# Chunked attention before two gated layers: heads traded in half a block, value products in four quadrants of the array

## The chip, the cores and the metric

The kernel runs on one core of a Trainium2 chip. The metric is the device time of one execution in microseconds (us): before the change 1714.94 us, the median of 3 runs (1713.28 to 1716.34). The profile is of one further execution.

## The reference, cut to what matters

```python
def _attn_ref(q, k, v):                       # each 8 batches x 8 heads x 576 rows x 64
    q_c, k_c, v_c = (x.reshape(B, H, S // 64, 64, D) for x in (q, k, v))   # chunks of 64 rows
    scores = (1.0 / np.sqrt(D)) * np.matmul(q_c, k_c.transpose(0, 1, 2, 4, 3))
    scores = scores - np.max(scores, axis=-1, keepdims=True)
    attn = np.exp(scores)
    attn = attn / (np.sum(attn, axis=-1, keepdims=True) + 1e-09)
    return np.matmul(attn, v_c).reshape(B, H, S, D)

x = attn.transpose(0, 2, 1, 3).reshape(4608, 512)                          # heads side by side
x = (1.0 / (1.0 + np.exp(-(x @ w_gate))) * (x @ w_val)) @ w_out            # 512 -> 1536 -> 512
h = x @ w2_in                                                              # 512 -> 2048
out = np.where(h >= 1, h, np.where(h <= -1, 0.0, (h + 1) ** 2 / 4)) @ w2_out
```

Each head attends within chunks of 64 rows alone, so a chunk of one head is a 64x64 score matrix, a softmax over its rows and a 64x64 value product. All matmuls of the two layers are computed as three products of a high and a low part each.

## The kernel before, in words

**Stages.** The 4608 rows are cut into nine blocks of 512. Blocks 0 to 3 and 5 to 8 are the first 512 rows of a batch each; block 4 (`REST`) holds the last 64 rows of all eight batches. In the first stage, TensorE goes through the blocks; for each it makes 24 projections of the block's attention output X (12 gate, 12 value), one to a *slot*: twelve matmuls of 128x512 (function `three`, L459 to L461). A sigmoid on ACT (L875) and a product on DVE (L878) follow, and the result goes to DRAM (`g_store`, L761). While block b is projected, the attention of block b + 1 is made between the projections, and the weights of the later layers are prepared on DVE, ACT and GpSimd (POOL) and spooled to DRAM (`w_load` L103 and L107, `w_low` L112, `w_bits`, `w_join`, `s_sums`, `s_split` L170, `s_spool` L182). The second layers follow later with other code, which the change doesn't touch.

**Attention of one pair of heads.** Eight heads make four pairs. The class `Whole` has a method for each step, named by one letter:
- `load`: q and k of the two heads, from DRAM, all issued on SP (L284; block 4 L263). In form "V" the partition is 32 times a group (head, half of the head's 64 columns) plus the row modulo 32, and each DMA fills one group of one of q and k: eight DMAs of 64 KB.
- `t`: DVE transposes 32x32 squares (L304), so that head h has its 64 columns on partition half h and the rows along the tile.
- `s` (S): 16 score matmuls of 64x64x64 in fp32, for each chunk and head, from partition half h (row group of the array) to the partition half of the chunk's parity (column group), into a bank for each head. One fp32 matmul is two instructions in the trace.
- `m`, `e`, `n`, `w`: row maximum and subtraction (DVE, L331 and L333), exponent (ACT, L338), sum and reciprocal (DVE, L343 to L346), scaling (POOL, L351).
- `p` (PT): four 128x128 transposes on TensorE (L357). `c`: ACT copies them from PSUM (L360).
- `o` (O): 16 value matmuls of 64x64x64 (L367): head h from partition half h to partition half h, into a bank of its own.
- `x`: ACT copies the two halves of 64x512 into X's high part (L375). `l`: DVE takes the low part (L380).
- `v_load`: two DMAs, one for each head (L297): key row within the chunk on the partitions of that head's half.

**The order is written out.** `later_block(b, starts, when)` gives for each pair a start slot and for each of the letters t s m e n w p c o x l an offset in slots; `at(slot, prio, ...)` files the step, and `emit(slot)` issues a slot's steps ahead of its projection, sorted by the fraction of the slot, then priority, then order of filing. s, p and o have priority 0, m, e, c and x 1, the others 3; loads have a fraction of 0.5. Each engine, SP too, works its own instructions in the order of issue. Pairs start 5 slots apart in block 1 (during block 0's projections) and 6 apart later; `load` stands two pairs ahead. The scores use banks b4 and b5, PT b6, O b6 and b7. Block 0's own attention comes before all projections, in an order written out in `ORDER` and `LOADS`, with forms "M", "V", "M", "T" for its four pairs; in M and T TensorE transposes rather than DVE.

Of the kernel before, what the change touches and what calls it, by code (L numbers as in the profile page):

```python
# [13 lines left out]
AF = mybir.ActivationFunctionType  # L14
ALU = mybir.AluOpType
# [14 lines left out]
def kernel(  # L30
# [15 lines left out]
    nc = tc.nc  # L46
    P = 128
    B, H, S, D = q.shape
# [3 lines left out]
    KT = DM // P  # L52
    CH = 64
    BS = 512
# [23 lines left out]
    def f32(t):  # L78
        return t.bitcast(F32)
# [138 lines left out]
    def x_tile(n=BS, name="x"):  # L218
        return pool["x"].tile([P, 2, n], F32R, tag="x", name=name, bufs=8)

    REST = NB // 2
    RS = S - BS

    def batch(blk):
        return blk - (blk > REST)

    NC = BS // P
    heads = [slice(h * D, (h + 1) * D) for h in range(2)]
    chunks = [slice(i * CH, (i + 1) * CH) for i in range(BS // CH)]

    class Whole:
# [7 lines left out]
        def bank(self, i, shape, name):  # L239
# [4 lines left out]
                self.nt += 1  # L244
            return ps.tile(shape, F32, tag=tag, name=name)

        def load(self, p):
            t = self.alloc("qk")
            how = self.how[p]
            if how == "V":  # L250

                t = t.rearrange("p i (t r) -> p i t r", r=32)
            elif how == "T":

                t = t.rearrange("p i (j h d) -> p i j h d", h=2, d=D)
            else:
                t = t.rearrange("p i (h j d) -> p i h j d", h=2, d=D)
            for i, src in enumerate((q, k)):
                if self.b == REST:
                    for g in range(4):  # L260
                        h, j = divmod(g, 2)
                        for c in range(RS // 32):
                            nc.sync.dma_start(  # L263
                                out=t[32 * g:32 * g + 32, i, c::RS // 32],
                                in_=src[:, 2 * p + h, BS + 32 * c:BS + 32 * c + 32, 32 * j:32 * j + 32].rearrange(
                                    "b i r -> i b r"
                                ),
                            )
                else:
                    rows = src[batch(self.b), 2 * p:2 * p + 2, :BS]  # L270
                    if how == "M":
                        nc.sync.dma_start(
                            out=t[:, i].rearrange("i h j d -> i h (j d)"),
                            in_=rows.rearrange("h (i j) d -> i h (j d)", j=NC),
                        )
                    elif how == "T":
                        for h in range(2):
                            nc.sync.dma_start(
                                out=t[:, i, :, h], in_=rows[h].rearrange("(i j) d -> i j d", j=NC)
                            )  # L280
                    else:
                        for g in range(4):
                            h, j = divmod(g, 2)
                            nc.sync.dma_start(  # L284
                                out=t[32 * g:32 * g + 32, i],
                                in_=rows[h, :, 32 * j:32 * j + 32].rearrange("(t i) r -> i t r", i=32),
                            )
            self.qk[p] = t

        def v_load(self, p):  # L290
            self.V[p] = t = self.alloc("vd").rearrange("p i (c e) -> p (i c) e", e=D)
            for h, hs in enumerate(heads):
                if self.b == REST:
                    rows = v[:, 2 * p + h, BS:].rearrange("b k d -> k b d")
                else:
                    rows = v[batch(self.b), 2 * p + h, :BS].rearrange("(c k) d -> k c d", k=CH)
                nc.sync.dma_start(out=t[hs, :BS // CH], in_=rows)  # L297

        def t(self, p):
            qk, how, ident = self.qk[p], self.how[p], kv_["ident"]  # L300
# [14 lines left out]
        def s(self, p):  # L315
            t = self.T[p]
            self.SP[p] = self.alloc("sp")
            banks = [self.bank(1 + h, [P, NC, CH], "S") for h in range(2)]
            for c, ts in enumerate(chunks):
                for h, hs in enumerate(heads):  # L320
                    nc.tensor.matmul(  # L321
                        banks[h][heads[c % 2], c // 2], lhsT=t[hs, 0, ts], rhs=t[hs, 1, ts], start=True, stop=True
                    )
            self.B["s", p] = banks

        def m(self, p):
            s = self.SP[p][:, 0].rearrange("p (g h k) -> p g h k", h=2, k=CH)
            m = cp.tile([P, 2, NC], F32, tag="m0", name="m", bufs=2)
            banks = self.B.pop(("s", p))
            for h, b in enumerate(banks):  # L330
                nc.vector.tensor_reduce(out=m[:, h], in_=b, axis=AX.X, op=ALU.max)  # L331
            for h, b in enumerate(banks):
                nc.vector.tensor_tensor(  # L333
                    out=s[:, :, h], in0=b, in1=m[:, h].unsqueeze(2).to_broadcast([P, NC, CH]), op=ALU.subtract
                )

        def e(self, p):
# [10 lines left out]
        def w(self, p):  # L348
            s = self.SP[p][:, 0].rearrange("p (g k) -> p g k", k=CH)
            r = self.B.pop(("r", p))  # L350
            nc.gpsimd.tensor_tensor(out=s, in0=s, in1=r.unsqueeze(2).to_broadcast([P, 2 * NC, CH]), op=ALU.mult)  # L351
# [9 lines left out]

        def o(self, p):

            banks = [self.bank(4 + h, [P, BS], "O") for h in range(2)]
            for c, ts in enumerate(chunks):
                for h, hs in enumerate(heads):
                    nc.tensor.matmul(  # L367
                        banks[h][hs, ts], lhsT=self.V[p][hs, c], rhs=self.SP[p][hs, 1, ts], start=True, stop=True
                    )
            self.B["o", p] = banks  # L370

        def x(self, p):
            t = X[self.b, p] = x_tile()
            for h, hs in enumerate(heads):
                nc.scalar.activation(t[hs, 0], self.B["o", p][h][hs], AF.Copy)  # L375

        def l(self, p):
            t = X[self.b, p]
            for (h, hs), b in zip(enumerate(heads), self.B.pop(("o", p))):
                nc.vector.tensor_tensor(out=t[hs, 1], in0=b[hs], in1=f32(t[hs, 0]), op=ALU.subtract)  # L380

    def first_block():
        ft = ps.tile([P, BS], F32, tag="b5", name="fill")
# [55 lines left out]
    def later_block(b, starts, when):  # L439

        bufs = {"qk": 3, "qkT": 1, "sp": 2, "vd": 2}

        def alloc(nm):
            cols = BS // 2 if nm == "vd" else BS
            return pool["u"].tile([P, 2, cols], F32, tag=nm, name=nm, bufs=bufs[nm])

        a = Whole(b, [None, "b4", "b5", "b6", "b6", "b7"], alloc, "V" * KT)
        for p, s0 in enumerate(starts):
            at(begun[-2] + 0.5, 5, a.load, p)
            begun.append(s0)  # L450
            at(s0 + 0.5, 5, a.v_load, p)
            for fn, dt in zip("tsmenwpcoxl", when):
                at(s0 + dt, {"s": 0, "p": 0, "o": 0, "m": 1, "e": 1, "c": 1, "x": 1}.get(fn, 3), getattr(a, fn), p)
# [22 lines left out]
    banks, B0, B1, OP, R_ = {}, {}, {}, {}, {}  # L476
# [271 lines left out]
    NS = 2 * F1  # L748
# [3 lines left out]
    def at(slot, prio, fn, *args):  # L752
        order[0] += 1
        ev.setdefault(int(slot // 1), []).append((slot % 1, prio, order[0], fn, args))
# [6 lines left out]
        nc.sync.dma_start(out=gT[b][f * P:(f + 1) * P, :], in_=sg)  # L761

    begun = [-6.5, -6]
    later_block(1, [5 * p for p in range(KT)], (0, 1, 1.5, 2, 3, 3, 5, 5.5, 7, 7.5, 8))
    for b in range(2, NB):
        later_block(
            b, [NS * (b - 1) + 6 * p - 6 for p in range(KT)], (0, 2, 3, 4, 5, 5.5, 7, 8, 9, 10, 11)
        )

    NW = 4  # L770
# [79 lines left out]
    with tc.manual_schedule():  # L850
        half = cp.tile([P, 1], F32, name="half")
# [69 lines left out]
```

## Time and profile before

| | us |
|---|---|
| median of 3 runs | 1714.94 |
| the profiled execution | 1715.51 |
| its span, first to last instruction | 1713.7 |
| TensorE matmuls busy (97% of the span) | 1668.6 |
| DVE busy | 1171.4 |
| ACT busy | 863.9 |
| GpSimd (POOL) busy | 833.8 |
| O, 1152 instructions of 64x64 (L367) | 45.1 |
| S, 1152 instructions of 64x64 (L321) | 25.9 |
| PT, 144 instructions of 128x128 (L357) | 22.8 |

Busy time of an engine is the union of its instructions' spans; the spans of TensorE's matmuls overlap, and their ends are modelled, so what a group costs is read from the starts of what stands before and behind it. PE is TensorE, PEld its weight loads, SPq the queue of SyncE on which DMAs are issued.

### The profile page before, as it was taken

The numbers are of one execution on the slowest core, as the hardware profiler recorded it, in microseconds if no ns is written. First come the engines' busy times: TensorE is split into PE (matmuls) and PEld (weight loads), VectorE is DVE, ScalarE is ACT, GpSimd is POOL, SyncE is SP. The second block draws the span as 40 slices with busy tenths as digits, with TensorE's granted clock in tenths as the row PEclk, the third lists the DMA queues.
The fourth block names the chain that finished last, engine by engine and source line by source line (L and its number), as shares of the span: only waits on it lengthen the run. The fifth ranks groups of instructions, "written<-read, shape, count | busy, mean of one in ns | idle before, by whom it ended". The sixth has DMA issues, their size and how long they took to land.

```text
span 1713.7 us, 29607 instructions
## 1 busy us (share of the span) xinstructions
PE 1668.6 (97%) x10658; PEld 1528.4 (89%) x10658; DVE 1171.4 (68%) x1727; ACT 863.9 (50%) x1560; POOL 833.8 (49%) x758
## 2 busy tenths in 40 slices
PE   6899999999999999999999999999999999999996
PEld 5678888888888888899999989999999999999996
DVE  5874555555555541297777767888787888887975
ACT  4664454445444541155555555555554545455542
POOL 2432444433434340177777754444350477677774
PEclk7999999999999999999999999999999999999998
DMA  8856768777668656634644653423329764455442
GB/s 203 218 134 163 213 172 239 228 201 235 212 200 230 212 188 231 217 122 141 226 142 148 246 221 133 155 104 148 148 107 340 281 215 116 107 156 154 115 111 38
DMA packets 386723, 307.11 MB, mean 179 GB/s; under 512 B 268944, under 2 KB 299664, under 8 KB 386576
## 3 DMA queue, kind: packets, MB, share of 16 engines
q1 hardware_dynamic: 386576, 305.22, 57.8%
q8 instruction: 84, 1.38, 0.3%
q14 instruction: 63, 0.52, 0.1%
HBM read 179.83 MB, written 125.30 MB: 178 GB/s over the span
## 4 chain that ended last, share of the span: by engine, by line
PE 86%; DVE 7%; SPq 2%; ACT 1%; issue 1%; POOL 1%; DMA 1%; ACTq 0%; DVEq 0%; POOLq 0%
PE P L460 17%; PE P L461 17%; PE P L459 16%; PE pr L459 11%; PE pr L461 11%; PE pr L460 11%; DVE z L492 3%; PE O L367 2%; PE S L321 1%; SPq L284 1%; DVE z L503 1%; PE PT L357 1%; POOL z L503 1%; DVE raw L118 1%; DVE raw L126 0%
## 5 line engine op out<-in xcount | busy, mean ns | idle before, releaser
L503 POOL TENSOR_TENSOR z<-z 128x384 fp32r<-128x384 f32 x308 | 357.2, 1184 | 313.3 <-ACT z L496 309.1
L460 PE MATMUL P<-z,w 128*128 128x384 f32 x1344 | 451.5, 336 | 8.4 <-DVE z L503 4.2
L459 PE MATMUL P<-z,w 128*128 128x384 f32 x1344 | 449.8, 335 | 0.8 <-ACT z L496 0.8
L461 PE MATMUL P<-z,w 128*128 128x384 f32 x1344 | 449.6, 335 | 0.0
L459 PE MATMUL pr<-x,w 128*128 128x512 f32 x864 | 347.8, 403 | 0.0
L461 PE MATMUL pr<-x,w 128*128 128x512 f32 x864 | 338.0, 391 | 0.0
L460 PE MATMUL pr<-x,w 128*128 128x512 f32 x864 | 337.4, 391 | 0.0
L496 ACT ACTIVATE z<-z 128x384 fp32r<-128x384 f32 x420 | 205.1, 522 | 180.3 <-DVE z L492 105.8
L878 DVE TENSOR_TENSOR sg<-pr,sg 128x512 f32<-128x512 f32 x108 | 74.6, 691 | 313.0 <-PE pr L461 144.5
L460 PEld LDWEIGHTS P<-z,w 128*128 128x128 f32 x1344 | 252.8, 188 | 13.6 <-POOL z L503 7.7
L503 POOL TENSOR_TENSOR op<-in,op 128x384 fp32r<-128x384 f32 x168 | 190.8, 1155 | 148.2 <-ACT op L496 147.8
L459 PEld LDWEIGHTS P<-z,w 128*128 128x128 f32 x1344 | 252.7, 188 | 1.3 <-ACT z L496 1.1
L461 PEld LDWEIGHTS P<-z,w 128*128 128x128 f32 x1344 | 252.8, 188 | 0.0
L459 PEld LDWEIGHTS pr<-x,w 128*128 128x128 f32 x864 | 162.6, 188 | 35.4
L461 PEld LDWEIGHTS pr<-x,w 128*128 128x128 f32 x864 | 162.5, 188 | 35.3
L460 PEld LDWEIGHTS pr<-x,w 128*128 128x128 f32 x864 | 163.0, 189 | 31.4
L496 ACT ACTIVATE op<-in 128x384 fp32r<-128x384 f32 x252 | 128.5, 524 | 112.8 <-PE P L461 60.7
L875 ACT ACTIVATE sg<-pr 128x512 f32<-128x512 f32 x108 | 64.5, 597 | 233.5 <-PE pr L461 226.7
L492 DVE TENSOR_TENSOR z<-z 128x384 f32<-128x384 f32 x200 | 169.9, 900 | 5.8 <-POOL z L503 5.8
L460 PE MATMUL P<-op,w 128*128 128x384 f32 x504 | 168.5, 334 | 0.1
L459 PE MATMUL P<-op,w 128*128 128x384 f32 x504 | 168.4, 334 | 0.0
L461 PE MATMUL P<-op,w 128*128 128x384 f32 x504 | 168.4, 334 | 0.0
(63 smaller groups left out, 2250.0 us busy)
## 6 DMA issues: line engine op xcount, KB each, us to landing
uT<-ua SPq DMA_DIRECT2D x96, 384.0 KB, 2.3
z<-uT SPq DMA_DIRECT2D x96, 384.0 KB, 4.2
gT<-sg SPq DMA_DIRECT2D x108, 256.0 KB, 2.4
in<-gT SPq DMA_DIRECT2D x72, 256.0 KB, 4.0
raw<-in_moe_w_out_dram SPq DMA_DIRECT2D x28, 512.0 KB, 5.3
w<-swi SPq DMA_DIRECT2D x28, 512.0 KB, 6.1
w<-swp SPq DMA_DIRECT2D x28, 512.0 KB, 6.8
swi<-st SPq DMA_DIRECT2D x24, 512.0 KB, 4.0
```

The costliest lines, as they stand in the source:

```text
L118: nc.vector.scalar_tensor_tensor(out=word(0, I32), in0=word(1, I32), scalar=-(2**31), in1=word(0, I32), op0=ALU.bitwise_and, op1=ALU.bitwi ...
L284: nc.sync.dma_start(out=t[32 * g:32 * g + 32, i], in_=rows[h, :, 32 * j:32 * j + 32].rearrange("(t i) r -> i t r", i=32),)
L321: nc.tensor.matmul(banks[h][heads[c % 2], c // 2], lhsT=t[hs, 0, ts], rhs=t[hs, 1, ts], start=True, stop=True)
L367: nc.tensor.matmul(banks[h][hs, ts], lhsT=self.V[p][hs, c], rhs=self.SP[p][hs, 1, ts], start=True, stop=True)
L459: nc.tensor.matmul(o, lhsT=ah, rhs=bh, start=first, stop=False, skip_group_check=open_)
L460: nc.tensor.matmul(o, lhsT=ah, rhs=bl, start=False, stop=False, skip_group_check=open_)
L461: nc.tensor.matmul(o, lhsT=al, rhs=bh, start=False, stop=last, skip_group_check=open_)
L492: (eng or nc.vector).tensor_tensor(out=op_src(p, key), in0=x, in1=y, op=ALU.subtract)
L496: nc.scalar.activation(o[:, 0], op_src(p, key), AF.Copy)
L503: eng.tensor_tensor(out=o[:, 1], in0=op_src(p, key), in1=f32(o[:, 0]), op=ALU.subtract)
L875: nc.scalar.activation(sg, go, AF.Sigmoid)
L878: nc.vector.tensor_tensor(out=sg, in0=vo, in1=sg, op=ALU.mult)
```

## The change

- In `load`, the blocks of form "V" other than block 4 get q and k with the heads traded in the second half of the block: rows 0 to 255 of head h go to partition half h, rows 256 to 511 to the other half (`swap`). For that each of the eight DMAs is cut in two.
- `s` writes head h to partition half h of the output (column group h) in all cases. The row group is where the head's rows lie: h in the first half of the block, the other one in the second. Where nothing is traded (block 4, and three pairs of block 0) it is h throughout. Banks go by h in the first half and by the other in the second.
- So PT has a chunk's parity as its partition half, where it had the head. `v_load` puts the key rows of two neighbouring chunks on 128 partitions, and `o` goes from the partition half of the parity (row group) to that of the head (column group), with a bank for each parity.
- `x` and `l` work on 128 partitions and 256 columns, two for a pair as before.
- The offsets: c moves into the slot of p, and o, x, l one slot forward. In blocks 2 to 8 o then stands at 8 and s of the next pair, six slots on, at 2 + 6; in block 1 at 6 and 1 + 5.

```diff
+        def swap(self, p):
+            return self.b != REST and self.how[p] == "V"
 ...
         def load(self, p):
 ...
-                        for g in range(4):
-                            h, j = divmod(g, 2)
-                            nc.sync.dma_start(
-                                out=t[32 * g:32 * g + 32, i],
-                                in_=rows[h, :, 32 * j:32 * j + 32].rearrange("(t i) r -> i t r", i=32),
-                            )
+                        n = 2 if self.swap(p) else 1
+                        step = BS // n
+                        for u in range(n):
+                            for g in range(4):
+                                h, j = divmod(g, 2)
+                                part = rows[h ^ u, u * step:(u + 1) * step, 32 * j:32 * j + 32]
+                                nc.sync.dma_start(
+                                    out=t[32 * g:32 * g + 32, i, u * step // 32:(u + 1) * step // 32],
+                                    in_=part.rearrange("(t i) r -> i t r", i=32),
+                                )
 ...
         def v_load(self, p):
 ...
-                    rows = v[batch(self.b), 2 * p + h, :BS].rearrange("(c k) d -> k c d", k=CH)
-                nc.sync.dma_start(out=t[hs, :BS // CH], in_=rows)
+                    rows = v[batch(self.b), 2 * p + h, :BS]
+                    nc.sync.dma_start(out=t[:, :, hs], in_=rows.rearrange("(g k) d -> k g d", k=P))
 ...
         def s(self, p):
 ...
-            for c, ts in enumerate(chunks):
-                for h, hs in enumerate(heads):
-                    nc.tensor.matmul(
-                        banks[h][heads[c % 2], c // 2], lhsT=t[hs, 0, ts], rhs=t[hs, 1, ts], start=True, stop=True
-                    )
+            for c in range(NC):
+                for u in range(2):
+                    for h, hs in enumerate(heads):
+                        rows, ts = heads[h ^ u if self.swap(p) else h], chunks[c + NC * u]
+                        nc.tensor.matmul(
+                            banks[h ^ u][hs, c], lhsT=t[rows, 0, ts], rhs=t[rows, 1, ts], start=True, stop=True
+                        )
 ...
         def o(self, p):
-            banks = [self.bank(4 + h, [P, BS], "O") for h in range(2)]
-            for c, ts in enumerate(chunks):
+            banks = [self.bank(4 + r, [P, NC, CH], "O") for r in range(2)]
+            for g in range(NC):
                 for h, hs in enumerate(heads):
-                    nc.tensor.matmul(
-                        banks[h][hs, ts], lhsT=self.V[p][hs, c], rhs=self.SP[p][hs, 1, ts], start=True, stop=True
-                    )
+                    at_ = (h ^ g // 2) * BS // 2 + g % 2 * P + h * CH
+                    for r, rs in enumerate(heads):
+                        nc.tensor.matmul(
+                            banks[r][hs, g], lhsT=self.V[p][rs, g, hs], rhs=self.SP[p][rs, 1, at_:at_ + CH],
+                            start=True, stop=True,
+                        )
 ...
         def x(self, p):
             t = X[self.b, p] = x_tile()
-            for h, hs in enumerate(heads):
-                nc.scalar.activation(t[hs, 0], self.B["o", p][h][hs], AF.Copy)
+            for r, b in enumerate(self.B["o", p]):
+                nc.scalar.activation(self.half(t, 0, r), b, AF.Copy)
+
+        def half(self, t, i, r):
+            return t[:, i].rearrange("e (g r q) -> e g r q", r=2, q=CH)[:, :, r]
 ...
-    later_block(1, [5 * p for p in range(KT)], (0, 1, 1.5, 2, 3, 3, 5, 5.5, 7, 7.5, 8))
+    later_block(1, [5 * p for p in range(KT)], (0, 1, 1.5, 2, 3, 3, 5, 5, 6, 6.5, 7))
     for b in range(2, NB):
         later_block(
-            b, [NS * (b - 1) + 6 * p - 6 for p in range(KT)], (0, 2, 3, 4, 5, 5.5, 7, 8, 9, 10, 11)
+            b, [NS * (b - 1) + 6 * p - 6 for p in range(KT)], (0, 2, 3, 4, 5, 5.5, 7, 7, 8, 9, 10)
         )
```

(`l` changes as `x` does; `m` writes its two results side by side rather than interleaved; block 4's values come with four DMAs of half the size instead of two.)

## Rows read from the trace of the kernel before

**Rows 1.** The page, part 4: the chain that ended last, by line.

```profile
PE P L460 17%; PE P L461 17%; PE P L459 16%; PE pr L459 11%; PE pr L461 11%; PE pr L460 11%; DVE z L492 3%; PE O L367 2%; PE S L321 1%; SPq L284 1%; DVE z L503 1%; PE PT L357 1%; POOL z L503 1%; DVE raw L118 1%; DVE raw L126 0%
```

**Rows 2.** Busy time by stretch: length, engines' busy us, granted clock, DMA share, GB/s.

```profile
38.00:118.00 80.00, 70.94 (x542) 56.25 (x539) 69.78 (x118) 51.47 (x75) 34.08 (x25) 0.96 0.75 188
140.00:640.00 500.00, 500.00 (x3671) 403.81 (x3670) 266.11 (x502) 248.98 (x371) 195.82 (x203) 1.00 0.71 209
```

**Rows 3.** Timeline of TensorE, one pair: start, us, engine, line, tiles, instructions.

```profile
190.66 0.39 PE L461 MATMUL pr<-x,w 128*128 128x512 f32 x1
190.97 0.69 PE L321 MATMUL S<-qkT 64*64 64x64 f32 x32
191.60 0.50 PE L459 MATMUL pr<-x,w 128*128 128x512 f32 x1
191.94 0.39 PE L460 MATMUL pr<-x,w 128*128 128x512 f32 x1
...
194.00 0.39 PE L460 MATMUL pr<-x,w 128*128 128x512 f32 x1
194.23 0.39 PE L461 MATMUL pr<-x,w 128*128 128x512 f32 x1
194.55 1.15 PE L367 MATMUL O<-sp,vd 64*64 64x64 f32 x32
195.63 0.50 PE L459 MATMUL pr<-x,w 128*128 128x512 f32 x1
195.97 0.39 PE L460 MATMUL pr<-x,w 128*128 128x512 f32 x1
...
213.52 1.15 PE L367 MATMUL O<-sp,vd 64*64 64x64 f32 x32
```

**Rows 4.** Timeline of all engines from 225 to 229 us.

```profile
225.62 0.60 PE L357 MATMUL PT<-ident,sp 128*128 128x128 f32 x4
225.82 0.60 ACT L875 ACTIVATE sg<-pr 128x512 f32<-128x512 f32 x1 [3.74 <-PE pr L461]
...
227.25 0.68 ACT L170 ACTIVATE st<-raw 128x512 fp32r<-128x512 f32 x1 [0.27 <-POOL raw L151]
...
227.83 0.58 ACT L360 ACTIVATE sp<-PT 128x512 f32<-128x512 f32 x1
...
228.92 0.29 PE L321 MATMUL S<-qkT 64*64 64x64 f32 x4
```

**Rows 5.** Groups by line: count, busy us, mean ns, idle before, releaser.

```profile
L380 DVE TENSOR_TENSOR x<-O,x 64x512 fp32r<-64x512 f32 x72 | 49.4, 685 | 10.5 <-ACT x L375 9.4
L375 ACT ACTIVATE x<-O 64x512 fp32r<-64x512 f32 x72 | 42.6, 592 | 6.9 <-PE O L367 5.5
L338 ACT ACT_TABLE_LOAD x32 | 41.1, 1283 | 1.9 <-DVE sp L333 1.4
L333 DVE TENSOR_TENSOR sp<-S,m 128x256 f32<-128x256 f32 x72 | 26.9, 415 | 0.0
```

**Rows 6.** Timeline of SP's DMA issues: a pair's k, and block 4's q.

```profile
208.94 2.08 SPq L284 DMA_DIRECT2D qk<-in_k_dram  x4
...
226.50 4.08 SPq L263 DMA_DIRECT2D qk<-in_q_dram  x8
```

**Rows 7.** Timeline of DVE, three moments; in brackets its idle time before.

```profile
11.26 0.71 DVE L304 STREAM_TRANSPOSE qkT<-qk 128x512 f32<-128x512 f32 x1 [1.60 <-DMA qk<-in_k_dram]
...
62.80 0.42 DVE L112 TENSOR_SCALAR raw<-raw 128x512 int32<-128x512 uint32 x1
...
259.01 1.28 DVE L112 TENSOR_SCALAR raw<-raw 128x512 int32<-128x512 uint32 x1 [0.19 <-DMA raw<-in_moe_w_out_dram]
```

**Rows 8.** Timeline of TensorE at the third S of block 1.

```profile
82.17 1.13 PE L321 MATMUL S<-qkT 64*64 64x64 f32 x32 [3.15 <-DVE qkT L304]
```

**Rows 9.** Timeline of SP: one weight load in block 0.

```profile
50.99 0.49 SPq L103 DMA_DIRECT2D raw<-in_moe_w_gate_dram  x1
```

**Rows 10.** DMA issues by line: count, KB each, median us to landing.

```profile
raw<-in_moe_w_gate_dram SPq DMA_DIRECT2D x12, 512.0 KB, 6.2
```

More of the change, by code (lines that the diff above doesn't have):

```diff
@@ L281, in load @@
                     else:
-                        for g in range(4):
-                            h, j = divmod(g, 2)
-                            nc.sync.dma_start(
-                                out=t[32 * g:32 * g + 32, i],
-                                in_=rows[h, :, 32 * j:32 * j + 32].rearrange("(t i) r -> i t r", i=32),
-                            )
+                        n = 2 if self.swap(p) else 1
[8 more added lines that the diff above has]
+                                )
             self.qk[p] = t
         def v_load(self, p):
-            self.V[p] = t = self.alloc("vd").rearrange("p i (c e) -> p (i c) e", e=D)
+            t = self.alloc("vd").rearrange("p i e -> p (i e)")[:, :NC * P]
+            self.V[p] = t = t.rearrange("p (g e) -> p g e", e=P)
             for h, hs in enumerate(heads):
                 if self.b == REST:
-                    rows = v[:, 2 * p + h, BS:].rearrange("b k d -> k b d")
-                else:
-                    rows = v[batch(self.b), 2 * p + h, :BS].rearrange("(c k) d -> k c d", k=CH)
-                nc.sync.dma_start(out=t[hs, :BS // CH], in_=rows)
+                    for c, cs in enumerate(heads):
+                        nc.sync.dma_start(
+                            out=t[cs, :, hs], in_=v[c::2, 2 * p + h, BS:].rearrange("g k d -> k g d")
+                        )
+                else:
+                    rows = v[batch(self.b), 2 * p + h, :BS]
+                    nc.sync.dma_start(out=t[:, :, hs], in_=rows.rearrange("(g k) d -> k g d", k=P))
         def t(self, p):
@@ L317, in s @@
             self.SP[p] = self.alloc("sp")
-            banks = [self.bank(1 + h, [P, NC, CH], "S") for h in range(2)]
-            for c, ts in enumerate(chunks):
-                for h, hs in enumerate(heads):
-                    nc.tensor.matmul(
-                        banks[h][heads[c % 2], c // 2], lhsT=t[hs, 0, ts], rhs=t[hs, 1, ts], start=True, stop=True
-                    )
+            banks = [self.bank(1 + r, [P, NC, CH], "S") for r in range(2)]
+            for c in range(NC):
[5 more added lines that the diff above has]
+                        )
             self.B["s", p] = banks
         def m(self, p):
-            s = self.SP[p][:, 0].rearrange("p (g h k) -> p g h k", h=2, k=CH)
+            s = self.SP[p][:, 0].rearrange("p (r c k) -> p r c k", r=2, k=CH)
             m = cp.tile([P, 2, NC], F32, tag="m0", name="m", bufs=2)
@@ L333, in m @@
                 nc.vector.tensor_tensor(
-                    out=s[:, :, h], in0=b, in1=m[:, h].unsqueeze(2).to_broadcast([P, NC, CH]), op=ALU.subtract
+                    out=s[:, h], in0=b, in1=m[:, h].unsqueeze(2).to_broadcast([P, NC, CH]), op=ALU.subtract
                 )
@@ L362, in o @@
         def o(self, p):
-            banks = [self.bank(4 + h, [P, BS], "O") for h in range(2)]
-            for c, ts in enumerate(chunks):
+            banks = [self.bank(4 + r, [P, NC, CH], "O") for r in range(2)]
+            for g in range(NC):
                 for h, hs in enumerate(heads):
-                    nc.tensor.matmul(
-                        banks[h][hs, ts], lhsT=self.V[p][hs, c], rhs=self.SP[p][hs, 1, ts], start=True, stop=True
-                    )
+                    at_ = (h ^ g // 2) * BS // 2 + g % 2 * P + h * CH
[3 more added lines that the diff above has]
+                            start=True, stop=True,
+                        )
             self.B["o", p] = banks
@@ L373, in x @@
             t = X[self.b, p] = x_tile()
-            for h, hs in enumerate(heads):
-                nc.scalar.activation(t[hs, 0], self.B["o", p][h][hs], AF.Copy)
+            for r, b in enumerate(self.B["o", p]):
+                nc.scalar.activation(self.half(t, 0, r), b, AF.Copy)
+        def half(self, t, i, r):
+            return t[:, i].rearrange("e (g r q) -> e g r q", r=2, q=CH)[:, :, r]
         def l(self, p):
             t = X[self.b, p]
-            for (h, hs), b in zip(enumerate(heads), self.B.pop(("o", p))):
-                nc.vector.tensor_tensor(out=t[hs, 1], in0=b[hs], in1=f32(t[hs, 0]), op=ALU.subtract)
+            for r, b in enumerate(self.B.pop(("o", p))):
+                nc.vector.tensor_tensor(
+                    out=self.half(t, 1, r), in0=b, in1=f32(self.half(t, 0, r)), op=ALU.subtract
+                )
     def first_block():
```

## The prediction

> **What bounds the kernel now.** First the page's chain of work that ended last, split by line: the value products of the attention (O, L367) hold 2%, its scores (S, L321) 1%, and most of the rest is TensorE's dense matmuls [rows 1]. Then busy time by stretch: from 140 to 640 us TensorE is busy for 500.00 of 500 us at granted clock 1.00, while DVE has 266, ACT 249 and POOL 196 [rows 2]. So in that stretch every microsecond taken off TensorE's queue comes off the time, and one put on another engine costs nothing as long as no wait reaches TensorE. From 38 to 118 us (block 0's projections) it is different: TensorE 70.9 and DVE 69.8 of 80 us, with pauses on TensorE [rows 2]. Last the timeline of TensorE over one pair [rows 3]: what a pair costs there, and how its groups sit between the projections.
>
> **What S and O cost.** Projections follow each other at 0.23 us (194.00, 194.23). Around O, from the last projection before it to the second one behind it, 195.97 - 194.23 = 1.74 us pass; less two pitches of 0.23 that leaves 1.28 us for O. For S it is 191.94 - 190.66 - 0.46 = 0.82 us [rows 3]. Both groups are 32 instructions on 64x64 tiles; the streams take 1.08 and 0.63 us. The code tells them apart: S goes round all four quadrants of the array (row group = head, column group = parity of the chunk), O only over two, since head h has row group h and column group h. So I read it as: each quadrant gets through its own work at one rate, and 16 turns of two quadrants take 1.08 us where 8 turns of four take 0.63. Eight turns are then 0.46 us, and what S costs beyond its turns, 0.82 - 0.46 = 0.36 us, is the change of tile shape on both sides (the gap of 0.32 ahead, and 0.34 between the first two projections behind, both against 0.23).
>
> **The change, part by part.**
> *Value products in four quadrants.* The new O goes over (row group = parity, column group = head) in just the order in which S goes now, with as many instructions, and each row group keeps a bank of its own. Below, S's 0.82 us is the end, as the same turns can't go faster; above, O's 1.28. I take 0.82: the pattern is S's. Gain 0.46 us an O.
> *Scores with heads traded in the second half.* The 28 pairs of blocks 1 to 3 and 5 to 8 keep four quadrants, in another order: row groups 0, 1, 1, 0 instead of 0, 1, 0, 1. Ends 0.82 and 1.28; I take 0.82, for the quadrants used count, not their order: no gain, no loss. The Trainium skill ("TensorE: Matmul & The Clock Gate", "Part 3: Packing small matmuls — row/col tiling") speaks against it: a weight load overlaps matmuls in flight only where the row group differs, and the new order has two seams in four without that. No row of before holds two neighbours in one row group; by that rule the scores go to the two-quadrant price, rival A below.
> *Scores not traded.* Four pairs of block 4 (the tails of all batches) and three of block 0 now have only two quadrants, since the output's half is the head. Price O's old 1.28, so 0.46 more each: 4 x 0.46 = 1.8 us lost in the dense stretch. Both row groups also write both banks in turn. If they had to take turns at that, the 16 turns became 32, 0.9 us more for each of the four, 3.7 us; I take nothing, as the two run in step and stand at different banks. (The Trainium skill, "TensorEngine Tiling (Array Packing)", "Restrictions and Gotchas", says that different row tiles cannot access one bank at once; by it those 3.7 us could come, and no row here shows such a case.)
> *O in the slot of the next pair's S.* In blocks 2 to 8 starts lie 6 slots apart, O moves from 9 to 8 and S of the next pair stands at 2 + 6 = 8; both have the first place in the slot, O ahead. Of 28 such pairs 27 find a partner; in block 1 three of four do (6 = 5 + 1). One group of 16 turns costs what O costs now, 1.28, instead of two at 0.82: 0.36 us saved each. Ends: 0 (a seam between O and S like that to a projection) and 0.36; I take 0.36, because both have the same tile shape.
> *Value copy c, one slot sooner.* c, the ACT copy that O waits for, now follows the transposes PT in their own slot, and O comes one slot after PT rather than two. Behind a waiting O stand the next pair's S and all projections. The slowest copy of the dense stretch: PT starts at 225.62, c runs from 227.83 to 228.41, since copies of the weight preparation (L170, 227.25) are queued ahead of it. The new O is due where S now starts, behind one slot of projections, at 228.92 [rows 4]. So even from its old place c is in time by 0.5 us, and from its new one, right behind the sigmoid that ends at 226.42, by well over a microsecond. I cost it at nothing; the cover is the slot of projections.
> *x and l on 128 partitions.* Two 64x512 instructions become two of 128x256. On DVE 685 ns become about the 415 of the 128x256 subtraction from PSUM, 0.54 us a pair; ACT's 592 ns fall likewise [rows 5]. Off the path in the dense stretch, so nothing there.
> *Twice as many loads.* A traded pair has 16 issues of half the size on SP instead of 8. Four of the old take 2.08 us (0.52 each); block 4 issues such halves already, 8 in 4.08 us (0.51) [rows 6]. So 16 x 0.51 - 8 x 0.52 = 4.0 us more of SP per pair of 18.97 us (O to O, 194.55 to 213.52 [rows 3]). Queued behind are weight loads, spools and stores. That block 4's sixteen are borne shows in the one wait near them: DVE stood 0.19 us for a weight at 259.01 [rows 7], and TensorE nowhere. v loads keep number and size.
>
> **The sum.** Dense stretch: 28 O x 0.46 = 12.9; 27 seams x 0.36 = 9.7; four plain S, -1.8. Together 20.8 us.
> First 118 us: on TensorE block 1's pairs give 4 x 0.46 + 3 x 0.36 = 2.9 us, but DVE is as full, and saves 4 x 0.54 = 2.2. There TensorE waits for DVE's transposes ahead of S, 3.15 us at 82.17 [rows 8]; O now goes into that wait. Against it: block 0's pair 1 has eight more issues, ahead of the load for which DVE already waits 1.60 us at 11.26 [rows 7], up to 4 us, of which later waits absorb some; and three pairs' loads stand in SP's queue ahead of the weight issued at 50.99 [rows 9] and used at 62.80 [rows 7]. With 6.2 us to landing [rows 10] it has 62.80 - 50.99 - 6.2 = 5.6 us of room, and two pairs' additions are 8.0: up to 2.4 us late, more if the third isn't hidden by transfers in progress. Between +5 and -6 I take a gain of 1, nearest to DVE's 2.2 less part of the delays.
> Total 21.8 us off the profiled execution's 1715.5, which is 1693.7; that one lies 0.6 above the median of the runs, so 1693 us.
>
> **Rivals.**
> A: the traded scores fall to the two-quadrant pace. For it: no row has this order. Against: pace goes by quadrants in both rows. 28 x 0.46 = 12.9 back: 1706 us.
> B: O and S in one slot save nothing. 9.7 back: 1703 us. For it: none joined in the rows; against: same tile shape, and S needs only transposes that are long done.
> C: SP's extra 4.0 us make weight loads late, DVE stands in its order and with it the products that free TensorE's banks. For it: the wait at 259.01 under just such loads; against: 0.19 us, and it reached no one. If one pair in seven waited the full 4.0: 4 x 4.0 = 16 back, 1709 us.
> D, the other side: c is late for O. If an exponent's two table loads of 1283 ns each (to its table and back to the sigmoid's) [rows 5] fall ahead of c, its end in the worst place moves from 2.79 to 5.36 us behind PT's start, against 3.30 at which O is due [rows 4]: 2.06 us of wait. In all 28 pairs that is 58 us, and the result 1693 + 58 = 1751 us. It is a loss from 21.8 / 28 = 0.78 us a pair on. Against it: the new place in ACT's queue is ahead of all but the sigmoid, and the exponent stands three slots earlier.
>
> **How the numbers follow.** Forecast 78%, with its own range 1688 to 1698 (the ends of the first 118 us); A 7%, B 6%, C 5%, D 4%. The range 1687 to 1705 holds the forecast and B, and stops short of A, C and D. About 0.2% (3.4 us) can be told from no change: faster 0.92, within it 0.03, slower 0.05, D and some unforeseen wait.
>
> **What would show it.** O's group with 32 instructions in 0.63 us, not 1.08; O and the next S as 64 instructions in about 1.08 between two projections; 18.15 us instead of 18.97 from O to O; block 4's S at 1.08; no pause ahead of O or PT from 140 us on; sixteen issues of about 0.5 us. Wrong would be a pause ahead of O (D), S at 1.08 in traded blocks (A), a gap between O and S (B), DVE waiting for weights with TensorE behind it (C), or block 0's projections starting more than 3 us later.

## The result and the profile after

The changed kernel takes 1698.22 us, the median of 4 runs (1696.02 to 1698.56), beside 1714.37 of the kernel before on the same chip (4 runs, 1713.28 to 1716.34). The ratio is 0.9902 with an interval of 0.9885 to 0.9919: 16 us faster, where 22 were forecast. The profiled execution took 1698.29 us, its span is 1696.4.

The page of the changed kernel, part 4: the chain that ended last, by line (O is now L383, S L335, PT L371, the projections L481 to L483).

```profile
PE P L482 17%; PE P L483 17%; PE P L481 17%; PE pr L481 10%; PE pr L483 10%; PE pr L482 10%; DVE z L514 2%; SPq L292 2%; DMA raw<-in_moe_w_gate_dram 1%; PE O L383 1%; PE S L335 1%; DVE z L525 1%; PE PT L371 1%; SPq L309 1%; POOL z L525 0%
```

O's share of the chain falls from 2% to 1%, and two queue items appear or grow: SP's q and k issues (L292, 2% where they had 1%) and landings of gate weights [rows 1]. Most of those come from the first 112 us of the chain, the rest from the pause told of below.

Busy time by stretch (length, engines' busy us, granted clock, DMA share, GB/s):

```profile
38.00:118.00 80.00, 69.17 (x550) 55.47 (x551) 67.47 (x119) 48.98 (x76) 34.15 (x26) 0.93 0.69 180
140.00:640.00 500.00, 497.06 (x3769) 407.41 (x3769) 249.96 (x507) 236.98 (x378) 196.46 (x203) 1.00 0.74 215
```

In [rows 2] the 500 us held 3671 matmul instructions of TensorE, now 3769: the work runs ahead. But 2.9 us of TensorE's time is now idle, and the first stretch has still more pauses than before (69.17 busy us, not 70.94).

The groups on TensorE, a pair of block 2:

```profile
189.73 0.39 PE L482 MATMUL pr<-x,w 128*128 128x512 f32 x1
189.96 0.39 PE L483 MATMUL pr<-x,w 128*128 128x512 f32 x1
190.28 0.69 PE L383 MATMUL O<-sp,vd 64*64 64x64 f32 x32
190.79 0.65 PE L335 MATMUL S<-qkT 64*64 64x64 f32 x32
191.37 0.50 PE L481 MATMUL pr<-x,w 128*128 128x512 f32 x1
191.71 0.39 PE L482 MATMUL pr<-x,w 128*128 128x512 f32 x1
```

Read as in [rows 3]: 191.71 - 189.96 - 0.46 = 1.29 us for O and S together, where O alone had 1.28 and S 0.82. From O to O 18.13 us pass (190.28 to 208.41), not 18.97. So the machine's part of the change is there in full.

The scores in block 4, which are not traded:

```profile
263.33 1.11 PE L335 MATMUL S<-qkT 64*64 64x64 f32 x32
264.37 0.50 PE L481 MATMUL pr<-x,w 128*128 128x512 f32 x1
```

S runs over two quadrants and takes 264.37 - 263.33 = 1.04 us, with both row groups writing both banks in turn.

To see where the time went, the span is cut at three places that can be read in every trace: the start of the first projection, the start of block 1's first projection, and the start of the second layers. The stretch between the last two is TensorE-bound ("dense" below). All in us, from one profiled execution each. In three pairs of kernels the dense stretch comes out alike to 0.1 us (before and e2, e4 and e9, e7 and e8, in the table at the end of the experiments), so a difference of some microseconds there is clear of noise:

| kernel | first projection | block 1's projections | second layers begin at | dense | end of span |
|---|---|---|---|---|---|
| before | 39.0 | 128.0 | 723.7 | 595.7 | 1713.7 |
| after | 39.7 | 129.9 | 708.7 | 578.8 | 1696.4 |

Of the 17.3 us, 16.9 come from the dense stretch; the start loses 1.9, and the second layers, which are the same code, come out 2.3 shorter (987.7, not 990.0; in the executions told of here they lie between 987.7 and 991.0, with no pattern that goes with the change). The forecast was 20.8 for the dense stretch and 1.0 for the start.

**The dense stretch: one pause.** The trace has one large wait of TensorE between 110 and 640 us. Its three sides, first TensorE:

```profile
391.29 0.39 PE L483 MATMUL pr<-x,w 128*128 128x512 f32 x1
394.62 1.13 PE L383 MATMUL O<-sp,vd 64*64 64x64 f32 x32 [2.94 <-ACT sp L374]
...
396.54 0.79 PE L481 MATMUL pr<-x,w 128*128 128x512 f32 x1
```

ACT ahead of it, behind the transposes PT on TensorE:

```profile
388.31 0.60 PE L371 MATMUL PT<-ident,sp 128*128 128x128 f32 x4
...
390.07 0.67 ACT L122 ACTIVATE raw<-raw 128x512 f32<-128x512 f32 x1 [6.40 <-DVE raw L118]
392.91 0.69 ACT L122 ACTIVATE raw<-raw 128x512 f32<-128x512 f32 x1 [2.18 <-DVE raw L118]
393.49 0.60 ACT L897 ACTIVATE sg<-pr 128x512 f32<-128x512 f32 x1
393.96 0.60 ACT L374 ACTIVATE sp<-PT 128x512 f32<-128x512 f32 x1
```

DVE and SP ahead of that:

```profile
388.88 0.43 DVE L112 TENSOR_SCALAR raw<-raw 128x512 int32<-128x512 uint32 x1 [6.08 <-DMA raw<-in_moe_w_in_dram]
```
```profile
374.91 5.51 SPq L292 DMA_DIRECT2D qk<-in_q_dram  x8
380.46 3.90 SPq L292 DMA_DIRECT2D qk<-in_k_dram  x8
384.41 1.00 SPq L103 DMA_DIRECT2D raw<-in_moe_w_in_dram  x2
```

Read from the bottom: two weight loads stand behind sixteen q and k issues (9.4 us, 0.59 each) and are issued at 384.41. DVE stands 6.08 us for the first of them. ACT stands 6.40 and 2.18 us for DVE at L122, a copy of the weight preparation. The sigmoid L897 and c (L374) are queued behind L122, although PT had started at 388.31, and O waits for c. Everything on TensorE is behind O. The pause also costs clock: O and S take 1.92 us from 394.62 to 396.54, where they take 1.09 from 190.28 to 191.37. The granted clock shows it, last but two in this row:

```profile
394.00:398.00 4.00, 3.38 (x68) 3.03 (x69) 2.26 (x6) 0.57 (x2) 2.83 (x4) 0.57 1.11 322
```

After some 3 us without matmuls the mean falls to 0.57, which is mostly the lower level of 1.2 GHz; in the 6 us before 394 and the 6 us after 398 it is 1.00. The three projection matmuls behind S still take 1.38 us (396.54 to 397.92), twice the usual 0.69. The whole event costs about 4.

**The start: SP sets the pace.** SP's issues for block 1's first two pairs and the next gate weight, and waits of DVE and TensorE:

```profile
30.95 8.95 SPq L292 DMA_DIRECT2D qk<-in_q_dram  x8
39.95 4.61 SPq L292 DMA_DIRECT2D qk<-in_k_dram  x8
44.60 3.90 SPq L292 DMA_DIRECT2D qk<-in_q_dram  x8
48.55 3.90 SPq L292 DMA_DIRECT2D qk<-in_k_dram  x8
...
62.37 0.45 SPq L103 DMA_DIRECT2D raw<-in_moe_w_gate_dram  x1
```
```profile
13.49 0.71 DVE L316 STREAM_TRANSPOSE qkT<-qk 128x512 f32<-128x512 f32 x1 [3.44 <-DMA qk<-in_k_dram]
...
46.45 0.71 DVE L316 STREAM_TRANSPOSE qkT<-qk 128x512 f32<-128x512 f32 x1 [2.49 <-DMA qk<-in_k_dram]
...
67.77 0.43 DVE L112 TENSOR_SCALAR raw<-raw 128x512 int32<-128x512 uint32 x1 [2.36 <-DMA raw<-in_moe_w_gate_dram]
```
```profile
47.22 1.13 PE L335 MATMUL S<-qkT 64*64 64x64 f32 x32 [3.05 <-DVE qkT L316]
```

The gate weight of [rows 9] is issued at 62.37, not 50.99. DVE waits 3.44 us for block 0's second pair where [rows 7] have 1.60, then 2.49 at block 1's first pair, with TensorE standing 3.05 behind it, and 2.36 for that gate weight. Where nothing holds it up, one issue costs about 0.49 us (3.90 / 8) whether it moves 32 KB or 64 (0.52, [rows 6]).

Off the path, x and l fell as forecast ([rows 5] had 592 and 685 ns):

```profile
L400 DVE TENSOR_TENSOR x<-O,x 128x256 fp32r<-128x256 f32 x72 | 26.9, 416 | 3.9 <-ACT x L392 3.9
...
L392 ACT ACTIVATE x<-O 128x256 fp32r<-128x256 f32 x72 | 23.6, 384 | 0.3 <-PE O L383 0.3
```

### The profile page after: what moved, and what is told of

Its sections match the earlier page's. It is cut to its first block, busy times and chain, and to the rows that moved or that the text cites. A ratio compares the mean times of both kernels' runs of the same rounds, so it can differ in the third digit from the quotient of the medians.

```text
span 1696.4 us, 29931 instructions
## 1 busy us (share of the span) xinstructions
PE 1642.7 (97%) x10658; PEld 1515.6 (89%) x10658; DVE 1146.3 (68%) x1727; ACT 843.1 (50%) x1560; POOL 836.3 (49%) x758
## 3 DMA queue, kind: packets, MB, share of 16 engines
q8 instruction: 84, 1.38, 0.3%
## 4 chain that ended last, share of the span: by engine, by line
PE 85%; DVE 6%; SPq 4%; DMA 2%; issue 1%; ACT 1%; POOL 0%; DVEq 0%; ACTq 0%; POOLq 0%
PE P L482 17%; PE P L483 17%; PE P L481 17%; PE pr L481 10%; PE pr L483 10%; PE pr L482 10%; DVE z L514 2%; SPq L292 2%; DMA raw<-in_moe_w_gate_dram 1%; PE O L383 1%; PE S L335 1%; DVE z L525 1%; PE PT L371 1%; SPq L309 1%; POOL z L525 0%
## 5 line engine op out<-in xcount | busy, mean ns | idle before, releaser
L481 PE MATMUL P<-z,w 128*128 128x384 f32 x1344 | 449.9, 335 | 1.2 <-ACT z L518 1.2
L483 PE MATMUL P<-z,w 128*128 128x384 f32 x1344 | 449.6, 335 | 0.0
L481 PE MATMUL pr<-x,w 128*128 128x512 f32 x864 | 345.4, 400 | 0.0
L483 PE MATMUL pr<-x,w 128*128 128x512 f32 x864 | 338.5, 392 | 0.0
L525 POOL TENSOR_TENSOR op<-in,op 128x384 fp32r<-128x384 f32 x168 | 191.2, 1157 | 148.3 <-ACT op L518 147.8
L482 PEld LDWEIGHTS P<-z,w 128*128 128x128 f32 x1344 | 252.8, 188 | 10.4 <-DVE z L525 5.2
L481 PEld LDWEIGHTS P<-z,w 128*128 128x128 f32 x1344 | 252.8, 188 | 1.7 <-ACT z L518 1.7
L483 PEld LDWEIGHTS P<-z,w 128*128 128x128 f32 x1344 | 252.9, 188 | 0.0
L483 PEld LDWEIGHTS pr<-x,w 128*128 128x128 f32 x864 | 163.2, 189 | 35.0
L481 PEld LDWEIGHTS pr<-x,w 128*128 128x128 f32 x864 | 163.3, 189 | 34.7
L897 ACT ACTIVATE sg<-pr 128x512 f32<-128x512 f32 x108 | 64.5, 597 | 233.8 <-PE pr L483 231.6
L483 PE MATMUL P<-op,w 128*128 128x384 f32 x504 | 168.4, 334 | 0.0
L481 PE MATMUL P<-op,w 128*128 128x384 f32 x504 | 168.4, 334 | 0.0
```

Source lines behind the costliest of these rows:

```text
L481: nc.tensor.matmul(o, lhsT=ah, rhs=bh, start=first, stop=False, skip_group_check=open_)
L482: nc.tensor.matmul(o, lhsT=ah, rhs=bl, start=False, stop=False, skip_group_check=open_)
L483: nc.tensor.matmul(o, lhsT=al, rhs=bh, start=False, stop=last, skip_group_check=open_)
L525: eng.tensor_tensor(out=o[:, 1], in0=op_src(p, key), in1=f32(o[:, 0]), op=ALU.subtract)
L897: nc.scalar.activation(sg, go, AF.Sigmoid)
```

## Experiments

Theory: the quadrants and the joint slot give what was forecast, and what is missing was lost to SP's doubled issues, at the start and once in the dense stretch. Rivals: the new offsets lose it, or the new order of the scores does.

Each was timed in 5 rounds beside the kernel before; results are told as the ratio to it, with its interval (e2 to e5 ran on one chip, e6 to e9 on another). "Dense" and "start" are the columns of the table above; the table at the end of this section has them all.

**e2_cut_loads.** The kernel before, with each q and k load cut in two and nothing traded.

```diff
-                        for g in range(4):
+                        n = 2 if how == "V" else 1
+                        step = BS // n
+                        for u in range(n):
+                            for g in range(4):
...
+                                part = rows[h, u * step:(u + 1) * step, 32 * j:32 * j + 32]
```

> The kernel before, with each of the eight q and k loads of a pair cut in two and nothing else changed (no trade, O and S as before). Theory SP: the change's shortfall against the forecast (the first 118 us 1.8 us longer instead of 1 shorter, one pause of 4.2 us at O near 394 us) comes from SP, which issues sixteen halves in 7.8 us instead of eight in 4.2. Then this kernel shows the same in the first 128 us, 2 to 4 us later than before, and perhaps a pause later on: 1716 to 1721 us. Rival: the shortfall comes from the new order of c, O and S on ACT and TensorE; then this one is 1714 us like before.

Measured: 1720.5 us, 1.0025 (1.0016 to 1.0034). Block 1 begins at 132.8, 4.8 us later than before; dense is 595.6, the 595.7 of before to 0.1. DVE at block 0's second pair:

```profile
13.20 0.71 DVE L308 STREAM_TRANSPOSE qkT<-qk 128x512 f32<-128x512 f32 x1 [3.46 <-DMA qk<-in_k_dram]
```

The wait of 3.46 us is the changed kernel's 3.44. Twice the issues cost the start, and with the offsets of before nothing after it.

**e3_old_offsets.** The changed kernel with the old tuples: c one slot behind PT, O, x, l a slot later, O no longer in S's slot.

```diff
-    later_block(1, ..., (0, 1, 1.5, 2, 3, 3, 5, 5, 6, 6.5, 7))
+    later_block(1, ..., (0, 1, 1.5, 2, 3, 3, 5, 5.5, 7, 7.5, 8))
-            b, ..., (0, 2, 3, 4, 5, 5.5, 7, 7, 8, 9, 10)
+            b, ..., (0, 2, 3, 4, 5, 5.5, 7, 8, 9, 10, 11)
```

> The changed kernel with the old offsets (c, o, x, l as before, so O and S in slots of their own). Theory: O and S in one slot save one change of tile shape, 0.36 us a pair in 27 + 3 pairs, 10 to 11 us; the pause at 394 us may go, since O then comes two slots behind PT (4 us): 1704 to 1709 us. Rival: the seam costs nothing and the four quadrants of O give all of the gain: 1698 us or less.

Measured: 1704.09 us, 0.9932 (0.9919 to 0.9944); dense 584.8, with no wait of O there. TensorE is busy for 500.00 us from 140 to 640.

So O's four quadrants less block 4's plain scores gave 595.7 - 584.8 = 10.9 us (forecast 12.9 - 1.8 = 11.1). The pause at 394 us needs the new offsets, which leave O one slot behind PT.

**e4_no_trade.** The changed kernel with no pair traded: eight whole loads a pair, all scores on two quadrants.

```diff
-            return self.b != REST and self.how[p] == "V"
+            return False
```

> The changed kernel without the trade: eight whole loads for a pair, and the scores of all pairs in two quadrants, O in four. Scores: 29 pairs x 0.47 us = 13.6 us more on TensorE. Theory SP: 5 to 6 us come back from the loads, so 1698 + 13.6 - 5.6 = 1706 us, with the first 128 us shorter than in the changed kernel by 2 us or more and no pause near 394 us. Rival (shortfall from the order on ACT and TensorE): 1711 us with the pause still there.

Measured: 1697.45 us, 0.9890 (0.9876 to 0.9904): as fast as the changed kernel. Dense is 585.2, without a pause, but block 1 begins at 120.4: 9.5 us earlier than in the changed kernel, and 7.6 earlier than before. Its trace at the place of the wait at 46.45:

```profile
39.78 1.30 DVE L316 STREAM_TRANSPOSE qkT<-qk 128x512 f32<-128x512 f32 x2
```

DVE does not wait there at all. The expectation let the loads give back 5.6 us in all and came out 8 us too high: the start alone gave back 9.5. The trade is a wash as it was made: it gains on S, and gives that back in the start and in the pause.

**e5_two_queues.** The changed kernel with the k halves issued on ACT's queue.

```diff
-                                nc.sync.dma_start(
+                                (nc.scalar if i else nc.sync).dma_start(
```

> The changed kernel with the halves of k issued on ACT's queue and those of q on SP's. Theory SP: SP's share falls to what it was before, the first 128 us and the pause at 394 us give back 5 to 8 us: 1690 to 1693 us. Rival 1: the sixteen halves are slow as transfers, whoever issues them: 1698 us. Rival 2: eight issues of 0.5 us make ACT late for the sigmoid and c, with pauses at O in many pairs: 1700 us and more.

Measured: 1747.62 us, 1.0178 (1.0159 to 1.0196). ACT in the dense stretch, with ACTq its own DMA issues:

```profile
169.68 5.16 ACTq L292 DMA_DIRECT2D qk<-in_k_dram  x8
174.88 0.60 ACT L897 ACTIVATE sg<-pr 128x512 f32<-128x512 f32 x1 [4.51 <-DMA qk<-in_k_dram]
175.38 0.59 ACT L374 ACTIVATE sp<-PT 128x512 f32<-128x512 f32 x1
```
```profile
176.02 0.69 PE L383 MATMUL O<-sp,vd 64*64 64x64 f32 x32 [3.49 <-ACT sp L374]
```

Eight issues take 5.16 us, the sigmoid L897 stands 4.51 us for them, c (L374) behind it, and O 3.49 for c: rival 2 of the expectation. Block 1 begins at 148.3 and dense is 609.6, against 129.9 and 578.8: an engine whose copies TensorE waits for is a bad place for these issues. It says nothing against SP as the cause, since it replaces one queue's delay by a worse one.

**e6_trade_from_2.** The changed kernel with heads traded only from block 2 on; the start is that of e4.

```diff
-            return self.b != REST and self.how[p] == "V"
+            return self.b > 1 and self.b != REST
```

> The changed kernel with the trade in blocks 2, 3 and 5 to 8 alone; block 0's pair 1 and block 1 load whole, and their scores go over two quadrants. Theory SP: of the 9.4 us by which the whole loads without any trade are ahead at the 288th projection matmul, most comes back, less 5 x 0.47 us for the scores: 1698 - 7 = 1691 us, or 1687 us if the pause near 394 us goes as well. Rival (what the trade costs lies in the dense stretch, in its order of quadrants or its banks): 1698 + 2 = 1700 us.

Measured: 1689.28 us, 0.9851 (0.9836 to 0.9866). Block 1 begins at 121.1, so the start's loss is gone with its halved loads; the pause is still there in the profiled execution (1694.01 us, the slowest of four; the others took 1688.86 to 1689.62):

```profile
385.67 1.13 PE L383 MATMUL O<-sp,vd 64*64 64x64 f32 x32 [2.74 <-ACT sp L374]
```

**e7_from_2_spread.** e6, with the second half's eight issues filed three slots after the first half's, so that what is queued behind can go in between.

```diff
-            at(begun[-2] + 0.5, 5, a.load, p)
+            if a.swap(p):
+                at(begun[-2] + 0.5, 5, a.load, p, (0,))
+                at(begun[-2] + 3.5, 5, a.load, p, (1,))
+            else:
+                at(begun[-2] + 0.5, 5, a.load, p)
```

> As the kernel with the trade from block 2 on, and the loads of a traded pair's second half issued three slots behind those of the first, so that SP never has sixteen in a row ahead of a weight load. Theory SP queue: the pause of 4.2 us near 394 us goes, 1687 us. Rival (the pause comes from transfers, the same bytes in the same packets): 1691 us, the pause stays.

Measured: 1684.34 us, 0.9824 (0.9811 to 0.9838): 14 us faster than the changed kernel, the fastest here. SP, and TensorE at the pair that paused:

```profile
363.14 2.15 SPq L300 DMA_DIRECT2D qk<-in_q_dram  x4
365.34 1.93 SPq L300 DMA_DIRECT2D qk<-in_k_dram  x4
367.31 2.24 SPq L103 DMA_DIRECT2D raw<-in_moe_w_in_dram  x2
```
```profile
381.80 0.69 PE L390 MATMUL O<-sp,vd 64*64 64x64 f32 x32
382.31 0.65 PE L342 MATMUL S<-qkT 64*64 64x64 f32 x32
```

The two weight loads now go out between the two halves (four q and four k each; the next half begins at 370.15), 14.5 us ahead of that O (381.80 - 367.31). In the changed kernel they went out 7.3 ahead of the time when O was due (394.62 - 2.94 - 384.41). O waits nowhere in the dense stretch, and dense is 574.5, against 580.0 in e6. The same issues of the same size, in another order: so the wait needs that order of SP's queue.

**e8_spread.** The changed kernel (all traded) with the loads spread in the same way.

> The changed kernel with the trade everywhere, and the second half's loads three slots behind the first's. Theory SP queue: the pause near 394 us goes (4.2 us), the first 128 us stay as long or get up to 3 us longer, since block 1's first pair gets its second half later: 1694 to 1697 us. Rival: the pause stays, 1698 us or more.

Measured: 1695.3 us, 0.9891 (0.9877 to 0.9904). Dense is 574.4 without a pause, but block 1 begins at 127.9. Spreading mends the dense stretch and leaves most of the start's loss; the whole time can't be told from the changed kernel's, since the intervals overlap.

**e9_cut_no_trade.** e4 with each load cut in two, so that it differs from the changed kernel in the scores' quadrants alone, and from e4 in the issues alone.

```diff
-                        n = 2 if self.swap(p) else 1
+                        n = 2 if how == "V" else 1
...
-                                part = rows[h ^ u, u * step:(u + 1) * step, 32 * j:32 * j + 32]
+                                part = rows[h, u * step:(u + 1) * step, 32 * j:32 * j + 32]
```

> The changed kernel without the trade (scores in two quadrants) but with the loads cut in two all the same. With the changed kernel and the one without trade and cut this tells the price of the cut from the gain of the trade. Theory: both add, the cut costs 13.6 us (9.4 at the start, 4.2 later), the four quadrants of the scores bring 13.1 to 13.6: 1697.5 + 13.6 = 1711 us. Rival (the trade's own order or banks cost time): 1698 us.

Measured: 1706.94 us, 0.9951 (0.9939 to 0.9964). The expectation was 4 us too high: the start's loss came (block 1 begins at 131.5, in e4 at 120.4), the pause did not (dense is 585.1, in e4 585.2). In its start the changed kernel's wait at 46.45 is back:

```profile
45.83 0.71 DVE L316 STREAM_TRANSPOSE qkT<-qk 128x512 f32<-128x512 f32 x1 [2.19 <-DMA qk<-in_k_dram]
```

SP and TensorE at the pair that paused in the changed kernel:

```profile
387.45 1.00 SPq L103 DMA_DIRECT2D raw<-in_moe_w_in_dram  x2
```
```profile
397.91 0.69 PE L383 MATMUL O<-sp,vd 64*64 64x64 f32 x32
```

So the sixteen issues in this order, with the new offsets, are not enough for the pause. With scores in two quadrants a pair takes TensorE 18.60 us (the O before starts at 379.31), not 18.13, and the weight loads go out 10.5 us ahead of O (397.91 - 387.45) instead of 7.3. In the changed kernel SP's batches begin 18.6 and 19.2 us apart there (337.11, 356.27, 374.91), so TensorE gains on SP.

All of them, in us as above:

| kernel | first projection | block 1's projections | dense | ratio |
|---|---|---|---|---|
| e2, before with cut loads | 40.6 | 132.8 | 595.6 | 1.0025 |
| e3, old offsets | 39.6 | 130.5 | 584.8 | 0.9932 |
| e4, no trade, whole loads | 36.2 | 120.4 | 585.2 | 0.9890 |
| e5, k issued on ACT | 37.2 | 148.3 | 609.6 | 1.0178 |
| e6, traded from block 2 | 36.2 | 121.1 | 580.0 | 0.9851 |
| e7, e6 with spread loads | 35.8 | 120.0 | 574.5 | 0.9824 |
| e8, all traded, spread loads | 38.0 | 127.9 | 574.4 | 0.9891 |
| e9, no trade, cut loads | 39.4 | 131.5 | 585.1 | 0.9951 |

## Why the prediction was right in direction and 5 us too low

**The quadrants: right.** O and S took what was forecast, and the dense stretch without its pause shows the whole sum: before less e8 is 595.7 - 574.4 = 21.3 us, forecast 20.8. The parts: O's quadrants 10.9 (e3); the joint slot, e3 less e8, 10.4, forecast 9.7; the traded scores, e9 less e8, 10.7, which is 23 S of 0.47 us (the first S of block 2 stands before the cut). Rivals A and B are out: row groups 0, 1, 1, 0 keep the four-quadrant pace (0.58 us from S to the next projection, 0.63 in [rows 3]), so the rule of the Trainium skill on weight loads that the prediction set against it costs nothing in this pattern; and two groups of one tile shape have no seam between them. Block 4's plain scores ran at 1.04 us, so two row groups at both banks in turn cost nothing either.

**The first 118 us: the step that failed.** The prediction put them at a gain of 1: DVE's 2.2 less a part of the delays, so about 1.2 of the 6.4 that it had priced (up to 4 for block 0's pair, up to 2.4 for the gate weight). Most of the 6.4 came. Block 1's first pair is transposed 2.7 us later than before (its second transpose ends at 47.16, not 44.50), and the gate weight is used 5.0 later (67.77, not 62.80 [rows 7]); block 1's start wins back 3.1 of that. The wait of 2.49 us for the first pair's own halves was in no term. DVE at that first pair, and SP at the start of block 1's loads, in the kernel before:

```profile
43.20 1.30 DVE L304 STREAM_TRANSPOSE qkT<-qk 128x512 f32<-128x512 f32 x2
```
```profile
28.51 7.21 SPq L284 DMA_DIRECT2D qk<-in_q_dram  x4
```

From there SP does almost nothing but issue q and k: 24 issues up to the gate weight at 50.99, in 22.5 us; after the change 48, from 30.95 to 62.37, in 31.4. The weight goes out 11.4 us later. It had 5.6 us of room and DVE is late itself by then, so DVE stands 2.36 for it, which is the size that the prediction gave this wait.

The experiments price both sides, and both lie outside the prediction's bounds of +5 and -6. With whole loads the rest of the change (O, x, l, the v loads, the offsets) gains 128.0 - 120.4 = 7.6 us up to block 1 (e4). Of these 2.8 come ahead of the first projection (39.0 and 36.2), where the prediction counted nothing. Cutting the loads takes 131.5 - 120.4 = 11.1 back (e9 less e4), 3.2 of it ahead of the first projection and 7.9 behind. That the traded kernel ends only 1.9 behind is luck: a gain and a loss that were both sized too small nearly cancel.

While SP is so occupied the transfers it feeds run short, as this window of the changed kernel and then of the untraded e4 shows (DMA share and GB/s at the end):

```profile
36.00:60.00 24.00, 19.45 (x122) 15.32 (x123) 17.83 (x32) 14.90 (x23) 10.96 (x9) 0.72 0.55 108
```
```profile
36.00:60.00 24.00, 21.49 (x160) 17.16 (x154) 21.74 (x37) 16.26 (x25) 10.81 (x8) 0.90 0.85 210
```

Half the rate, at a lower share: over most of this window the transfers wait for SP's issuing, not SP for them. That may also be why the same cut costs only 4.8 us in the kernel before (e2): with cut loads both kernels begin block 1 at about the same time (132.8 and 131.5), whatever O and x cost, so the gain that the new O would bring can't show. That last is argued from the two times; which wait sets each of them was not traced one by one.

**Rival C came, once.** SP's extra issues did make weight loads late and DVE stand, as C has it. But the way to TensorE was another than the banks: DVE held up ACT's L122, and c stood behind L122. The prediction held c safe, as "ahead of all but the sigmoid"; it read that from one place of the old trace [rows 4], where the copy ahead of c was L170. It didn't ask what the sigmoid itself stands behind. It cost 4.4 us: dense 578.8 instead of 574.4 (e8). With the start's 2.9 beyond its term that is 7.3; the dense stretch gave 0.5 more than forecast without it and the second layers 2.3, so 17.3 us came off the span where 21.8 were forecast. It takes three things together, each shown by a kernel without it that has no wait of O in the dense stretch: the new offsets (without them e3), the sixteen issues in a row (e7, e8), and the traded scores, by which TensorE goes through a pair faster than SP (e9).

**D did not come in the dense stretch.** The exponent's tables never fell ahead of c there: c ends 1.3 to 2.2 us behind PT's start, against 3.30 at which O is due, and 6.25 behind it in the one wait above. In the start O now waits for c (10.1 us in the whole trace, the last columns here, of which 2.9 are that one wait). At 85.11, with 2.79, something like D is part of it: ACT has loaded the sigmoid's table at 81.58 (1.28 us), ahead of sigmoid and c:

```profile
L383 PE MATMUL O<-sp,vd 64*64 64x64 f32 x1152 | 26.0, 229 | 10.1 <-ACT sp L374 10.1
```

## What to carry to other kernels

A change that cuts transfers in two is to be priced by the queue that issues them: list everything that the queue does between two landings that someone needs, at the start above all, where one queue feeds the whole pipeline. The same change can be worth much in one stage and cost as much in another; make it stage by stage (e6), and file the added issues apart (e7), so that what stands behind them can pass. When a step is moved closer to its consumer, follow its queue back over what stands ahead of it to the transfers which those wait for, in the worst place of the trace and not in a typical one.

## What the runs showed of the hardware that was not expected

- An issue on SP takes 0.49 us for 32 KB as for 64 KB (0.52) in the best rows, but not everywhere: at the start of block 1's loads 8 halves take 8.95 us (1.12 each, at 30.95), and 4 whole ones 7.21 before the change (1.80 each, at 28.51). What holds them up there is not shown. On ACT eight halves take 5.16 us, and what is queued behind them on ACT waits.
- A pause of some 3 us, with TensorE busy at full clock before and after, was enough to bring the granted clock to the lower of its two levels for the work behind it: O and S took 1.92 us rather than 1.09, and the next three projection matmuls 1.38 rather than 0.69.
- Two neighbouring matmuls in one row group, with different column groups, cost nothing: traded S takes 191.37 - 190.79 = 0.58 us to the next projection, where S took 0.63 in the order of before (191.60 - 190.97 [rows 3]).
